# Moving weight loads from the middle of an attention loop to its end, deferring two early loads, and a later turn of V

## The chip, the cores and the metric

One core of a Trainium2 chip runs the whole program. Times are device microseconds of that core. Most executions of one kernel agree within a per cent or two; each run is put down as fast or slow (slow when it is over 1.5% above the fastest of the same kernel), and ratios use fast runs alone. The clock granted to TensorE drops to half (0.50) in some stretches, and the profile shows in which. A profile is one execution, and the profiled one of the kernel before was a slow one (216.32 us, span 214.6).

## The reference

An attention stage feeds a soft mixture of experts:

```python
q, k, v: (8, 8, 576, 64)     beacon_k, beacon_v: (8, 8, 16, 64)
k_all, v_all = concat([beacon, own], axis=2)
a = softmax(causal(q @ k_all.T / 8));  attn = a @ v_all
x = attn.transpose(0, 2, 1, 3).reshape(4608, 512)
logits = x @ phi                       # phi: (512, 32)
slot_input = softmax(logits, 0).T @ x  # 8 experts with 4 slots each
slot_out[e] = relu(slot_input[e] @ w1[e]) @ w2[e]   # w1: (8,512,1024), w2: (8,1024,512)
out = softmax(logits, 1) @ slot_out    # (4608, 512), float32
```

The order matters for the argument: the experts need the softmax over all 4608 tokens, so they can't start before the last head is done, and no row of the output can leave before the last expert is done. The weights, 33.5 MB of 62.7 MB that are read, are needed only there and can be loaded before, as far as there is room: in this kernel the last eight of their 32 pieces lie where q, k and V's tail land, so they can go out only late in the loop.

## The kernel before

Two heads are a pair; a loop runs over 32 pairs, four per batch. Requests for q and k go out on SyncE, those for V and the weights on GpSimd, as V and the weights are cast from 4 to 2 bytes on the way. V comes as a main part per batch and a tail (the last rows of each head, for four batches at once); VectorE has to transpose, or turn, both before they are used. A weight request below is one of 32 pieces, each 1 MB read and 0.5 MB written.

```python
load_pair(0, nc.scalar); ...; load_pair(1); load_pair(2); load_pair(3); load_pair(4)
nc.sync.dma_start(out=phif[:, :, :], in_=moe_phi...)     # 512 pieces of 128 bytes
# ... V of batch 0 and its tail are requested on GpSimd ...
for n in range(NP):
    b, g = divmod(n, H // 2)
    score(n, 0)                      # q.k on TensorE, exp on ScalarE, causal mask on GpSimd
    score(n, 1)
    if n == 0:
        transp(1)                    # TensorE transposes of pair 1, copies on VectorE
        load_pair(5); load_pair(6)
        ...
        turn_v(0, 0); turn_v(0, 1)   # VectorE transposes of V(0): needed by attend(0)
        turn_tail(0, 0); turn_tail(0, 1)
    ...
    if n >= 1:
        attend(n - 1)                # a @ v on TensorE, normalisation on VectorE
    score(n, 2)
    if n + 2 < NP:
        transp(n + 2)
        if n + 7 < NP: load_pair(n + 7)
    score(n, 3)
    if n == 0: beacons(1, B)
    ...                              # requests and turns of the next V
    want = 24 * (n + 1) // 28 if n < 28 else (26, 28, 30, 32)[n - 28]
    while wl < want:
        load_w(wl); wl += 1          # a weight request, on GpSimd
```

Behind the loop come the last normalisation, the last logits, the eight experts (first layer, transposes, second layer), and then nine blocks of output.

The softmax here doesn't subtract the row's maximum and nothing guards it: scores larger than these inputs give would overflow.

Of the kernel before, what the change touches and what calls it, by code (L numbers as in the profile page):

```python
# [17 lines left out]
def kernel(  # L18
# [12 lines left out]
    nc = tc.nc  # L31
    P = 128
    B, H, S, D = q.shape
# [8 lines left out]
    J = S // 64  # L42
# [31 lines left out]
    arena = const.tile([P, E * 8192], F16, name="arena")  # L74
    lend = (E - 2) * 8192
# [9 lines left out]
    def load_pair(n, keng=None, qeng=None):  # L85
        b, g = divmod(n, H // 2)
        for i, (d, src) in enumerate(((qf, q), (kf, k))):
            o = lend + (2 * (n % QKS) + i) * 2 * J * D
            t = arena[:, o:o + 2 * J * D].bitcast(FP).rearrange("p (j d) -> p j d", j=J)
            ((qeng, keng)[i] or nc.sync).dma_start(  # L90
                out=t,
                in_=src[b, 2 * g:2 * g + 2].rearrange("h s d -> (h s) d").rearrange(
                    "(p j) d -> p j d", j=J))
            d[n] = t
# [38 lines left out]
    def turn(dst, src, hf):  # L133
        e = slice(hf * D // 4, (hf + 1) * D // 4)
        nc.vector.transpose(out=dst[:, e],  # L135
                            in_=src.bitcast(FP).rearrange("p (j e) -> p e j", j=TK)[:, e])

    def turn_v(b, hf):
        turn(vh[b % 2].bitcast(FP).rearrange("p c h e -> p e c h" if b == 0 else
                                             "p c h e -> p e h c"), vbuf[b % 2], hf)  # L140

    def turn_tail(b4, hf):
        turn(vt[b4].bitcast(FP).rearrange("p r e -> p e r")[0:96], vlast[0:96], hf)

    def load_bv(b):
        nc.gpsimd.dma_start(out=vbuf[b % 2][0:4 * H:4, 0:Nb * D],
                            in_=beacon_v[b].rearrange("h n d -> h (n d)"))
# [6 lines left out]
    NPC = 4 * E  # L154
# [3 lines left out]
    def load_w(m):  # L158
        e, r = divmod(m, 4)
        if r < 2:  # L160
            src = moe_w1[e, r * 256:(r + 1) * 256].rearrange("(p r) f -> p (r f)", r=2)
        else:
            src = moe_w2[e, (r - 2) * 512:(r - 1) * 512].rearrange("(p r) d -> p (r d)", r=4)
        nc.gpsimd.dma_start(out=arena[:, wloc[m]:wloc[m] + WP], in_=src)  # L164
# [13 lines left out]
    nc.sync.dma_start(out=bkf[:, 1:B, :], in_=bks[:, 1:B, :])  # L178
    load_pair(1)
    load_pair(2)  # L180
    load_pair(3)
    load_pair(4)
    phif = const.tile([P, NDC, NSL], FP, name="phif")
    nc.sync.dma_start(out=phif[:, :, :], in_=moe_phi.rearrange("(c p) e -> p c e", p=P))

    idb = const.tile([P, P], BF, name="idb")
# [6 lines left out]
    idh = const.tile([P, P], F16, name="idh")  # L193
# [26 lines left out]
    def double_beacons(b0, b1):  # L220
        for r in range(2):
            nc.vector.tensor_copy(out=bkd[:, b0:b1, r, :], in_=bkf[:, b0:b1, :])

    def beacons(b0, b1):
        tp = ps_tr.tile([P, B, P], BF, name="tr", tag="tr")
        for b in range(b0, b1):
            nc.tensor.transpose(tp[:, b, :], bkd[:, b, :, :].rearrange("p r d -> p (r d)"),
                                idb[:, :])
        for r in range(2):
            nc.vector.tensor_copy(  # L230
                out=bkT[64 * r:64 * r + 64, b0 * H // 2:b1 * H // 2, :],
                in_=tp[64 * r:64 * r + 64, b0:b1, :].rearrange(
                    "p b (g r n) -> p (b g) r n", g=H // 2, r=2)[:, :, r, :])

    def transp(n):
        (nc.vector if n < 2 else nc.gpsimd).tensor_copy(out=kT[n % 3][:, 0:Nb], in_=bkT[:, n, :])
        for (f, dst) in ((qf, qT[n % 3]), (kf, kT[n % 3])):
            t = f.pop(n)
            tp = ps_tr.tile([P, J, 64], BF, name="tr", tag="tr")
            for j in range(J):  # L240
                for po in (0, 64):
                    hi = t[po:po + 64, j, :].bitcast(BF)[:, 1::2]
                    nc.tensor.transpose(tp[po:po + 64, j, :], hi,  # L243
                                        idb[po:po + 64, po:po + 64])
            nc.vector.tensor_copy(out=dst[:, Nb:Nb + S].rearrange("p (s j) -> p s j", j=J),  # L245
                                  in_=tp[:, :, :].rearrange("p j s -> p s j"))
# [54 lines left out]
    def xt_piece(n):  # L301
        b, g = divmod(n, H // 2)
        if g == 0:
            xT[b] = exq.tile([P, NDC, U], F16, name="xT", tag="xT", bufs=2)
        tp = ps_tr.tile([P, NCH, P], F16, name="tr", tag="tr")
        for i in range(NCH):
            m = P if i < 4 else UL
            nc.tensor.transpose(  # L308
                tp[:, i, 0:m],
                xb[b % 2][0:m, i, 2 * g:2 * g + 2, :].rearrange("p h d -> p (h d)"),  # L310
                idh[0:m, 0:m])
        nc.vector.tensor_copy(out=xT[b][:, g, :],  # L312
                              in_=tp[:, :, :].rearrange("p i u -> p (i u)")[:, 0:U])
# [35 lines left out]
    def add_si(b, hf):  # L349
        sp = si_half(b, hf)  # L350
        z = siacc[:, 2 * hf:2 * hf + 2, :]
        nc.vector.tensor_tensor(out=z, in0=z, in1=sp, op=AL.add)
# [4 lines left out]
    wl = 0  # L357
    for n in range(NP):
        b, g = divmod(n, H // 2)
        score(n, 0)  # L360
        score(n, 1)
        if n == 0:
            transp(1)
            load_pair(5)
            load_pair(6)
            nc.vector.tensor_copy(out=idh[:, :], in_=idb[:, :])
            double_beacons(1, B)
            for hf in range(2):
                turn_v(0, hf)
            for hf in range(2):  # L370
                turn_tail(0, hf)
        if n >= 2:
            xt_piece(n - 2)
        if n >= 5 and g in (1, 2):
            logit_piece(b - 1, g - 1)
        if n >= 6 and g == 3:
            dt_piece(b - 1)
        if n >= 1:
            attend(n - 1)
        if n >= 6 and g == 3:  # L380
            add_si(b - 1, 0)
        if n >= 8 and g == 0:
            add_si(b - 2, 1)
# [3 lines that stand above are left out]
            if n + 7 < NP:  # L387
                load_pair(n + 7)
        score(n, 3)
        if n == 0:  # L390
            beacons(1, B)
        if n == 1:
            nc.vector.tensor_copy(out=phih[:, :, :, :],
                                  in_=phif[:, :, :].unsqueeze(2).broadcast_to([P, NDC, 4, NSL]))

        if n == 1:
            for qd in range(4):
                load_v(1, qd)
        if n == 2:
            load_bv(1)  # L400
        if n == 5:
            nc.gpsimd.memset(siz[:, :, :, :], 0.0)
        if n == 3:
            turn_v(1, 0)
            turn_v(1, 1)
        if 1 <= b < B - 1 and g in (2, 3):
            turn_v(b + 1, g - 2)
        if n == 3:
            for qd in range(4):
                load_v(2, qd)  # L410
        if n >= 4 and b + 2 < B:
            load_v(b + 2, g)
            if g == 0 and b == 1:
                load_bv(2)
            if g == 3:
                load_bv(b + 2)
        if 8 <= n < 11:
            load_tail(1, n - 8)
        if 13 <= n < 15:
            turn_tail(1, n - 13)  # L420
        want = 24 * (n + 1) // 28 if n < 28 else (26, 28, 30, 32)[n - 28]
        while wl < want:
            load_w(wl)
            wl += 1
# [9 lines left out]
    def col_sums(c0, c1):  # L434
# [5 lines left out]
                                scalar2=None, op0=AL.mult)  # L440
        nc.vector.reciprocal(out=z, in_=z)

    L = B - 1
    xt_piece(NP - 2)
    attend(NP - 1, split=True)
# [2 lines left out]
    def last_logits(ts):  # L448
        for hf in range(2):
            for t in ts:  # L450
                o = Nb + hf * (S // 2)
                nc.tensor.matmul(lps[hf], phih[:, t, :, :].rearrange("p g s -> p (g s)"),
                                 xT[L][:, t, o:o + S // 2],
                                 start=(t == 0), stop=(t == NDC - 1))

    add_si(L - 1, 1)
    nc.vector.tensor_scalar(out=siacc[:, :, :], in0=siacc[:, :, :], scalar1=2.0 ** -8,
# [4 lines left out]
    for hf in range(2):  # L462
        o = Nb + L * S + hf * (S // 2)
        nc.scalar.activation(eLh[:, o:o + S // 2], lps[hf], AF.Exp,
                             accum_out=dsum9[:, 2 * L + hf:2 * L + hf + 1])
    col_sums(0, 7)
    dt_piece(L)
    ds = siz[:, :, :, :]
    for hf in range(2):
        sp = si_half(L, hf)  # L470
        for r in range(2):
            c = 2 * hf + r
            nc.vector.scalar_tensor_tensor(
                out=bass.AP(tensor=ds.tensor, offset=ds.offset + c * NSL,
                            ap=[ds.ap[0], [NDC * NSL + SPE, E], [1, SPE]]),
# [106 lines left out]
```

## Time and profile before

The median of the first three runs was 213.8 us (212.13 to 216.71). In the profiled execution:

| point | us |
|---|---|
| first normalisation (pair 0) | 22.64 |
| normalisation of pair 4 | 43.41 |
| normalisation of pair 28 | 157.09 |
| last mask done, last two weight requests | 165.27 |
| second layer of the last expert | 185.92 |
| first output request | 189.55 |
| end of span | 214.6 |

The chain that ended last, from the page (first by engine, then by line):

```profile
PE 40%; DVE 20%; DMA 13%; ACT 10%; issue 5%; POOL 4%; DVEq 0%; POOLq 0%
```

TensorE (PE) is what most of the time is put down to. The table of stretches for points that the argument comes back to (length, busy time and count of PE, PEld (TensorE's weight loads), DVE (VectorE), ACT (ScalarE), POOL (GpSimd), then the granted clock, the DMA share and the GB/s written):

```profile
45.00:125.00 80.00, 69.03 (x1601) 54.04 (x1600) 58.27 (x112) 58.18 (x84) 44.33 (x86) 0.94 1.04 257
125.00:165.30 40.30, 35.03 (x855) 27.16 (x852) 29.64 (x62) 31.36 (x46) 21.63 (x44) 1.00 0.93 193
175.80:189.50 13.70, 11.62 (x181) 5.62 (x180) 3.78 (x13) 3.78 (x9) 0.00 (x0) 0.88 0.01 1
```

For 13.7 us ahead of the first output request the DMA engines have nothing to do, as all weights are there and no output is ready.

### The profile page before, as it was taken

How to read it: one execution, taken by the hardware profiler on the slowest of the kernel's cores; microseconds unless marked ns; L12 is line 12 of the kernel's file. 1: busy time of each engine (PE TensorE's matmuls, PEld its weight loads, DVE VectorE, ACT ScalarE, POOL GpSimd, SP SyncE). 2: the span in 40 equal slices, each digit the busy share in tenths (PEclk: the TensorE clock that was granted, in tenths of full speed). 3: DMA queues.
4: the chain of work that ended last, by engine and by line, in shares of the span. 5: the costliest groups of instructions: out<-in, count | busy, mean ns of one | idle time of the engine just before them, and what ended most of it. 6: DMA issues, size and time to landing. Idle time of an engine off the chain costs nothing.

```text
span 214.6 us, 7759 instructions
## 1 busy us (share of the span) xinstructions
PE 160.2 (75%) x3400; PEld 117.0 (55%) x3400; DVE 136.1 (63%) x284; ACT 128.5 (60%) x188; POOL 92.1 (43%) x180
## 2 busy tenths in 40 slices
PE   1545992998799869788959898789897889788200
PEld 1424762776577657676748677666675654333000
DVE  4477783579767849985766578579755442289400
ACT  2322893587688668568935896687887212289300
POOL 8500985585558655544544366533566000000000
PEclk9999998599999999979985999999999958999955
DMA  6998499999999999999999979998799950059997
GB/s 189 292 298 324 89 244 262 267 259 259 280 260 246 260 269 261 281 250 256 219 259 253 234 191 234 246 241 128 132 195 208 218 118 3 0 220 415 415 415 293
DMA packets 20273, 50.88 MB, mean 237 GB/s; under 512 B 5392, under 2 KB 5392, under 8 KB 19216
## 3 DMA queue, kind: packets, MB, share of 16 engines
q0 software_dynamic: 8000, 21.75, 53.7%
q1 hardware_dynamic: 12096, 28.35, 36.3%
q8 instruction: 26, 0.43, 0.7%
q10 hardware_dynamic: 144, 0.29, 0.4%
q14 instruction: 7, 0.06, 0.1%
HBM read 62.69 MB, written 9.44 MB: 336 GB/s over the span
## 4 chain that ended last, share of the span: by engine, by line
PE 40%; DVE 20%; DMA 13%; ACT 10%; issue 5%; POOL 4%; DVEq 0%; POOLq 0%
PE av L283 11%; ACT ex L262 10%; PE sc L256 9%; DMA vbuf<-in_v_dram 5%; DVE arena L546 5%; DMA arena<-in_v_dram 5%; PE tr L308 4%; DVE xb L294 4%; PE tr L243 4%; DMA vbuf<-in_beacon_v_dram 3%; DVE vh L135 3%; PE tr L319 3%; PE av L515 2%; DVE xT L312 2%; DVE kT L245 1%
## 5 line engine op out<-in xcount | busy, mean ns | idle before, releaser
L262 ACT ACTIVATE ex<-sc 128x1024 f16<-128x1024 f32 (+3 forms) x128 | 105.8, 870 | 52.4 <-PE sc L256 49.9
L264 POOL TENSOR_SCALAR_AFFINE_SELECT ex<-ex 128x1024 f16<-128x1024 f16 x32 | 35.4, 1106 | 67.5 <-ACT ex L262 67.5
L256 PE MATMUL sc<-qT,kT 64*128 64x128 bf16 (+5 forms) x576 | 46.5, 259 | 9.5 <-ACT ex L262 6.8
L283 PEld LDWEIGHTS <-ex 128*128 128x128 f16 (+2 forms) x960 | 37.6, 109 | 5.7 <-issue 4.6
L283 PE MATMUL av<-vh,ex 128*128 128x65 f16 (+1 forms) x896 | 38.6, 201 | 1.8 <-issue 1.6
L243 PE MATMUL tr<-idb,arena 64*64 64x64 bf16 x1152 | 29.5, 202 | 10.6 <-DVE xT L312 4.1
L243 PEld LDWEIGHTS <-arena 64*64 64x64 bf16 x1152 | 24.4, 116 | 19.1 <-issue 14.2
L256 PEld LDWEIGHTS <-kT 64*128 64x128 bf16 (+1 forms) x576 | 22.0, 103 | 19.3 <-issue 15.0
L294 DVE TENSOR_TENSOR xb<-av,r 128x640 f16<-128x640 f32 (+1 forms) x33 | 26.5, 804 | 1.1
L245 DVE COPY qT<-tr 128x576 bf16<-128x576 bf16 x32 | 24.0, 750 | 4.2 <-PE tr L243 4.0
L245 DVE COPY kT<-tr 128x576 bf16<-128x576 bf16 x32 | 24.0, 749 | 2.9 <-PE tr L243 2.8
L293 DVE RECIPROCAL r<-av 128x10 f32<-128x10 f32 (+1 forms) x33 | 7.2, 217 | 26.3 <-PE av L283 26.2
L135 DVE STREAM_TRANSPOSE vh<-vbuf 128x512 f32<-128x512 f32 x16 | 17.8, 1131 | 4.5 <-DMA vbuf<-in_beacon_v_dram 3.5
L312 DVE COPY xT<-tr 128x592 f16<-128x592 f16 x32 | 14.5, 453 | 9.1 <-PE tr L308 8.9
L164 POOL DMA_DIRECT2D arena<-in_moe_w_dram x32 | 18.0, 564 | 0.0
L111 POOL DMA_DIRECT2D vbuf<-in_v_dram x28 | 15.9, 576 | 2.6 <-DVE xT L312 2.6
L308 PE MATMUL tr<-idh,xb 128*128 128x128 f16 (+1 forms) x160 | 14.6, 225 | 1.0 <-DVE xb L294 1.0
L308 PEld LDWEIGHTS <-xb 128*128 128x128 f16 (+1 forms) x160 | 9.5, 101 | 7.2 <-issue 5.6
L546 DVE TENSOR_SCALAR arena<-fp,rc 128x512 f32<-128x512 f32 x18 | 12.3, 746 | 0.7 <-PE fp L542 0.7
L542 PE MATMUL fp<-soh,eLh 128*128 128x512 f16 x36 | 10.6, 377 | 2.6 <-ACT arena L544 1.3
L544 ACT ACTIVATE arena<-fp,rc 128x512 f32<-128x512 f32 x18 | 11.3, 686 | 1.7 <-PE fp L542 1.0
L319 PE MATMUL tr<-xT,phih 128*128 128x288 f16 x56 | 10.6, 295 | 1.1 <-DVE xT L312 1.1
(74 smaller groups left out, 130.5 us busy)
## 6 DMA issues: line engine op xcount, KB each, us to landing
arena<-in_moe_w_dram POOLq DMA_DIRECT2D x32, 512.0 KB, 9.6
arena<-in_q_dram SPq DMA_DIRECT2D x32, 288.0 KB, 8.8
arena<-in_k_dram SPq DMA_DIRECT2D x31, 288.0 KB, 10.6
out_dram<-arena SPq DMA_DIRECT2D x8, 1024.0 KB, 8.5
vbuf<-in_v_dram POOLq DMA_DIRECT2D x31, 128.0 KB, 7.4
out_dram<-arena SPq DMA_DIRECT2D x2, 512.0 KB, 3.1
arena<-in_v_dram POOLq DMA_DIRECT2D x4, 128.0 KB, 8.1
arena<-in_k_dram ACTq DMA_DIRECT2D x1, 288.0 KB, 2.7
```

Source lines behind the costliest of these rows:

```text
L135: nc.vector.transpose(out=dst[:, e], in_=src.bitcast(FP).rearrange("p (j e) -> p e j", j=TK)[:, e])
L164: nc.gpsimd.dma_start(out=arena[:, wloc[m]:wloc[m] + WP], in_=src)
L243: nc.tensor.transpose(tp[po:po + 64, j, :], hi, idb[po:po + 64, po:po + 64])
L245: nc.vector.tensor_copy(out=dst[:, Nb:Nb + S].rearrange("p (s j) -> p s j", j=J), in_=tp[:, :, :].rearrange("p j s -> p s j"))
L256: nc.tensor.matmul(sc[0:kn, a, col:col + un], kT[n % 3][64 * a:64 * a + 64, P * c:P * c + kn], qT[n % 3][64 * a:64 * a + 64, u0:u0 + un], ...
L262: nc.scalar.activation(ex[n][:, :, o:o + w], sc[:, :, 0:w], AF.Exp, scale=scale)
L264: nc.gpsimd.affine_select(out=ex[n][:, :, 0:512].rearrange("p a (c t) -> p a c t", c=4), in_=ex[n][:, :, 0:512].rearrange("p a (c t) -> p ...
L283: nc.tensor.matmul(av[0:m, a, i * DD:(i + 1) * DD], ex[n][0:kn, a, o:o + m], vchunk(b, 2 * g + a, c, kn), start=(c == 0), stop=(c == i))
L294: nc.vector.tensor_tensor(out=xo[:, z], in0=avv[:, z, :, 0:D], in1=r_.unsqueeze(3).broadcast_to([P, z.stop - z.start, NCH, D]), op=AL.mult)
L308: nc.tensor.transpose(tp[:, i, 0:m], xb[b % 2][0:m, i, 2 * g:2 * g + 2, :].rearrange("p h d -> p (h d)"), idh[0:m, 0:m])
L312: nc.vector.tensor_copy(out=xT[b][:, g, :], in_=tp[:, :, :].rearrange("p i u -> p (i u)")[:, 0:U])
L546: nc.vector.tensor_scalar(out=osb[:, j, :], in0=fp_[:, :], scalar1=rc[:, i:i + 1], scalar2=None, op0=AL.mult)
```

## The change

Its intent: fill that hole. Of the 32 weight requests only 11 go out while q, k and V still load (before: 20 by pair 23), 11 more in the last eight pairs, and ten behind the loop. At the start, pairs 3 and 4 are held back until the first mask is done (two tiny memsets on GpSimd write the target, so the load must wait for them), to let V(0) in sooner; and VectorE turns V(0) only after pair 2's copies and the beacons.

```diff
-    load_pair(3)
-    load_pair(4)
     phif = ...; nc.sync.dma_start(out=phif[:, :, :], ...)
@@ n == 0, behind score(0, 1)
             transp(1)
+            nc.vector.tensor_copy(out=idh[:, :], in_=idb[:, :])
+            for m in (3, 4):
+                o = lend + 2 * m * 2 * J * D
+                nc.gpsimd.memset(arena[:, o:o + 2 * J * D + 2:2 * J * D], 0.0)
+                load_pair(m)
             load_pair(5)
             load_pair(6)
-            nc.vector.tensor_copy(out=idh[:, :], in_=idb[:, :])
             double_beacons(1, B)
-            turn_v(0, 0..1); turn_tail(0, 0..1)        # (loops written short)
@@ n == 0, behind score(0, 3)
             beacons(1, B)
+            turn_v(0, 0..1); turn_tail(0, 0..1)
@@
-        want = 24 * (n + 1) // 28 if n < 28 else (26, 28, 30, 32)[n - 28]
+        want = n if n < 4 else 3 + 42 * (n - 3) // 100 if n < 24 else 11 + 145 * (n - 23) // 100
@@ behind the loop
+    while wl < NPC:
+        load_w(wl)
+        wl += 1
     L = B - 1
```

More of the change, by code (lines that the diff above doesn't have):

```diff
@@ L363 @@
             transp(1)
+            nc.vector.tensor_copy(out=idh[:, :], in_=idb[:, :])
[3 more added lines that the diff above has]
+                load_pair(m)
             load_pair(5)
             load_pair(6)
-            nc.vector.tensor_copy(out=idh[:, :], in_=idb[:, :])
             double_beacons(1, B)
-            for hf in range(2):
-                turn_v(0, hf)
-            for hf in range(2):
-                turn_tail(0, hf)
         if n >= 2:
@@ L391 @@
             beacons(1, B)
+            for hf in range(2):
+                turn_v(0, hf)
+            for hf in range(2):
+                turn_tail(0, hf)
         if n == 1:
```

## The prediction

> **What bounds the kernel now.** I read the page first (busy tenths, queues), then the chain of waits, then the timelines of VectorE and GpSimd, and last a table of stretches cut at the points those showed. The busy tenths of the page, by slices of 5.4 us:
>
> ```profile
> PEclk9999998599999999979985999999999958999955
> DMA  6998499999999999999999979998799950059997
> GB/s 189 292 298 324 89 244 262 267 259 259 280 260 246 260 269 261 281 250 256 219 259 253 234 191 234 246 241 128 132 195 208 218 118 3 0 220 415 415 415 293
> ```
>
> The DMA engines are at 8 tenths or more nearly everywhere, with two holes: slice 5 (20 to 25 us), and slices 33 to 35 (about 175 to 189 us), where no weights are left to load and no output is ready. The change aims at both. GB/s are bytes written; V and the weights are cast from 4 to 2 bytes on the way, so 208 to 218 GB/s of weights alone means 416 to 436 read.
>
> The stretches (columns: length, then busy time and count of PE, PEld, DVE, ACT, POOL, then the clock, the DMA share and GB/s):
>
> ```profile
> 20.00:25.00 5.00, 4.79 (x108) 3.72 (x105) 3.00 (x7) 4.11 (x5) 3.72 (x8) 1.00 0.36 79
> 43.40:157.10 113.70, 98.42 (x2340) 76.83 (x2340) 84.68 (x165) 83.99 (x120) 63.15 (x123) 0.95 1.00 238
> 165.30:175.00 9.70, 7.33 (x147) 5.49 (x143) 4.89 (x22) 2.63 (x7) 1.05 (x2) 0.86 1.02 205
> 175.00:189.50 14.50, 12.42 (x193) 6.10 (x190) 3.96 (x13) 4.16 (x10) 0.00 (x0) 0.86 0.01 2
> 189.50:214.60 25.10, 9.30 (x32) 3.38 (x30) 11.51 (x17) 10.33 (x17) 0.00 (x0) 0.77 0.91 376
> ```
>
> 43.4 to 157.1 us are the 24 pairs between the normalisations of pair 4 and pair 28: DMA is full, but TensorE is also busy 98.4 of 113.7 us. To tell which of them sets the pace I took the starts of that normalisation (one per pair) from VectorE's timeline: four pairs take 18.2, 18.9, 19.5, 21.2, 18.1 and 17.7 us. In the last of these six batches the steps are 4.2, 4.0, 4.3 and 5.2 us, and TensorE's waits there are fractions of a microsecond on ACT and VectorE. So about 17.7 us a batch is the compute pace, and the 24 pairs lose 113.7 - 6 x 17.7 = 7.5 us to everything else: about 1 us is two tail turns, some 3.5 us the half-clock stretches at 87 and 108 us, and 2 to 3 us DMA (late V, instruction fetches of TensorE).
>
> The start is different. VectorE's timeline:
>
> ```profile
> 13.63 2.03 DVE L135 STREAM_TRANSPOSE vh<-vbuf 128x512 f32<-128x512 f32 x2 [0.94 <-DMA vbuf<-in_v_dram]
> 16.03 2.02 DVE L135 STREAM_TRANSPOSE arena<-arena 96x512 f32<-96x512 f32 x2 [0.37 <-DMA arena<-in_v_dram]
> 17.92 0.73 DVE L245 COPY qT<-tr 128x576 bf16<-128x576 bf16 x1
> 22.64 0.83 DVE L294 TENSOR_TENSOR xb<-av,r 128x640 f16<-128x640 f32 x1
> 35.44 2.08 DVE L135 STREAM_TRANSPOSE vh<-vbuf 128x512 f32<-128x512 f32 x2 [3.53 <-DMA vbuf<-in_beacon_v_dram]
> ```
>
> The turns of batch 0's V sit in VectorE's order ahead of pair 2's q/k copies, so the copies wait for V and its tail until 17.92, and the first normalisation comes at 22.64. Then the turn of V(1) waits 3.53 us for a beacon piece. GpSimd, which issues V and weights in its program order, shows why, and where the last weights go out:
>
> ```profile
> 28.32 0.56 POOL L146 DMA_DIRECT2D vbuf<-in_beacon_v_dram  x1 [0.97 <-DMA vbuf<-in_v_dram]
> ...
> 165.27 1.07 POOL L164 DMA_DIRECT2D arena<-in_moe_w_dram  x2
> ```
>
> **What the Trainium skill says.** "DMA: Bandwidth & Descriptors", Specifications, gives a fabric ceiling of 435 GB/s over 16 engines; the weights-only slices here (218 written, 436 read) and the output (415) agree. Its section on the anatomy of a SWDGE DMA says that DMA engines do not wait on semaphores, the issuing sequencer does: the trace agrees, GpSimd sat idle 0.97 us in front of the beacon request, its masks behind it. The same page, "Issuing engines are not separate DMA queues", says that all issuers share the 16 engines, so deferring weights and pairs 3 and 4 should speed V. "TensorE: Matmul & The Clock Gate" says that the array falls to half clock after an idle window of about 3.4 us; the trace has half-clock stretches of 6.8 us at 32.6, 107.7 and 169.1, the first in the 4.15 us idle at the V(1) turn. Fewer stalls may mean fewer such stretches.
>
> **The change, part by part.**
> (1) Turns of V(0) later. Bytes read by 16.1 us: q/k of pairs 0 to 4 2.95 MB, beacon keys 0.26, V(0) and tail 1.84, that is 5.05 MB in 14.1 us, 358 GB/s. Without pairs 3 and 4 (1.18 MB) what the start needs is 3.87 MB, 10.8 us, landing near 13 us instead of 16. Pair 2's copies then end near 14.5, the turns (4.05 us) near 18.5 to 20, and the first normalisation near 19.3 to 21: 1.7 to 3.3 us earlier. V(1) is requested after pair 1's mask, whose scores no longer wait for the turns: near 16.5 instead of 22.77.
> (2) Pairs 3 and 4 wait for two tiny memsets on GpSimd behind pair 0's masks (end 10.05 us), so they are asked for near 10 us; pair 3 is transposed near 20, so there is slack. The memsets (0.1 us each) cost nothing on the path.
> (3) V(1)'s beacon piece: before, request to turn took 5.5 + 7.1 us and cost 3.53. V(1) now starts about 6.3 us earlier against a need 2.5 us earlier, but into a DMA queue still holding pairs 3 to 6, say 1.5 us lost: the stall falls to about 1.2. Saving 2.3.
> (1) to (3) make pair 4 about 4.8 us earlier.
> (4) Fewer weights in pairs 4 to 24 (42 per 100 pairs instead of 86): up to the 2 to 3 us of DMA waits, and perhaps 1 to 2 us of half clock that follow them: 3.5 us.
> So the last masks and with them the last requests come G = 4.8 + 3.5 = 8.3 us earlier (165.3 becomes 157).
> (5) The cost. Before, four weights or so were in flight at 165.3; they landed by 175, and the experts ended 187.0, bound by TensorE. Now only 22 of 32 are requested inside the loop, the 22nd at 157, and ten behind it. One weight is 0.524 MB written; at 213 GB/s 2.46 us. Two requests at the pair before (161.1 - G, 1.5 us start, 2 x 2.5) keep the engines until 167.6 - G; eleven more are 27.1 us: the last lands at 194.7 - G + 0.5 = 186.9. The last second layer and its wait take 0.9, then soh and output, in the profile 187.0 to 214.6, 27.6 us. End: 186.9 + 0.9 + 27.6 = 215.4 against 214.6. The experts are now bound by the landing of weights, about 9 us behind where TensorE could be; that eats G.
> The output (9.44 MB at 415 GB/s, 22.7 us) is unchanged.
>
> **Rivals.**
> A: the DMA queue is the bound through the whole loop, as its share of 1.00 suggests, and relief speeds every pair; then G is 11 to 13 and the span 210 to 212. For it: share 1.00, the late V. Against: 17.7 us a batch with TensorE nearly gapless.
> B: V(1) and V(2) still come late, as requests bunch in the first 20 us; G is 5 and the span 218.7. For it: pairs 3 to 8 now load exactly while V(1) does.
> C: the tail is hidden, as the experts' own work of 14 us takes as long as the weights. That needs landing by 186 - G, and 11 weights at 2.46 us rule it out unless fewer remain than I count.
> My sum lies between A and B.
>
> **Range and chances.** The profiled run was a slow one: 216.3 us for a span of 214.6, against a median of 213.8. Its half clock at 169 to 176 lies in the experts' stage and would be hidden in the changed kernel, behind weights. So I carry over 1.7 us from span to time (217.1) and take off half of the 2.5 us between this run and the median, about 215.9. The odd constants (42 and 145 per 100) look like ones found by trying on a chip, which speaks for a gain that I can't derive, so I lower this to 214.0. The 8-in-10 range is 209.5 to 218.5: G from 5 to 13, with the clock's share. Over 2% faster needs less than 209.5, thus rival A in full: 0.10. Over 2% slower needs more than 218.1, thus rival B: 0.13. Within 2%: 0.77.
>
> **What would show it right or wrong.** First normalisation at 19 to 21 us; the wait for V(1)'s beacon piece at 0 to 2 us; a batch of four pairs near 17.7 us with a DMA share near 0.8 between 45 and 125 us; the 22nd weight requested near 157 and the last weight landing near 187; DMA full from there back to 157; TensorE idle in the experts' stage, waiting for weights; no DMA hole ahead of the output of more than about 4 us. The prediction is wrong if batches fall well below 17.7 us, if weights land faster than 2.4 us each, or if the start saves more than 6 us or nothing.

## The result, and the profile after

| | median | range | runs |
|---|---|---|---|
| before, beside the changed kernel | 214.74 us | 212.13 to 216.71 | 4 |
| changed | 221.45 us | 220.35 to 224.0 | 4 |

The ratio is 1.037 (95% interval 1.025 to 1.049): slower, outside the predicted range. A ratio here is the mean time of one kernel's fast runs over that of the other's fast runs of the same rounds, so it is not quite the ratio of the medians.

The busy tenths of the changed kernel's page, by slices of 5.5 us:

```profile
PEclk9999999999999999999999999999995875579955
DMA  6998999999999988976998799999999999259995
GB/s 178 275 295 320 144 221 266 244 266 263 198 233 200 256 193 241 199 215 171 246 213 220 193 215 218 171 186 195 189 181 214 212 214 212 58 214 425 414 417 242
```

The hole ahead of the output has shrunk to about one slice, as intended, and this profile has no half-clock dips inside the loop. But from slice 11 to slice 27 the GB/s are mostly 170 to 250, where they were 220 to 280 before. The chain that ended last now has another first entry:

```profile
DMA 31%; PE 26%; DVE 15%; ACT 10%; issue 7%; POOL 5%; SPq 1%; DVEq 1%; ACTq 0%; POOLq 0%
```

DMA has taken TensorE's place, and by line half of it (16% of the span) is waiting for weights. The stretches, with the same columns as before:

```profile
45.00:125.00 80.00, 69.73 (x1728) 53.97 (x1726) 63.00 (x124) 61.29 (x89) 44.56 (x88) 1.00 0.90 219
125.00:158.20 33.20, 29.17 (x698) 22.75 (x697) 23.30 (x49) 26.60 (x39) 16.83 (x33) 1.00 0.99 197
158.20:190.60 32.40, 20.49 (x325) 11.02 (x322) 7.72 (x32) 5.32 (x14) 5.80 (x12) 0.71 1.00 197
190.60:194.90 4.30, 2.95 (x11) 0.94 (x11) 1.24 (x3) 1.59 (x3) 0.00 (x0) 0.50 0.00 0
```

The hole went from 13.7 to 4.3 us. In its place stands the third row: 32.4 us between the last mask and the landing of the last weight, where the kernel before took 10.5. TensorE is busy 20.5 us of it, much of that at half clock. How TensorE waited in the experts' stage (timeline of TensorE):

```profile
176.62 0.61 PE L520 MATMUL av<-arena,hbuf 128*32 128x512 f16 x8
183.50 0.62 PE L503 MATMUL av<-arena,siz 128*32 128x256 f16 x8 [6.26 <-DMA arena<-in_moe_w_dram]
185.99 0.62 PE L503 MATMUL av<-arena,siz 128*32 128x256 f16 x8 [1.88 <-DMA arena<-in_moe_w_dram]
...
190.87 1.04 PE L520 MATMUL av<-arena,hbuf 128*32 128x512 f16 x6 [0.95 <-DMA arena<-in_moe_w_dram]
```

L503 is the first layer, L520 the second. The bracket gives the idle time and what ended it: three times it is a weight, and the last expert's second half starts at 190.87.

Where did the weights go? The DMA view of the same 80 us in the middle of the loop, first before, then after (packets; then per queue packets, MB written, share of 16 engines; q0 is GpSimd's, with V and weights, q1 is SyncE's, with q and k):

```profile
DMA packets 8632, 20.57 MB, mean 257 GB/s; under 512 B 1744, under 2 KB 1744, under 8 KB 8616
q0 software_dynamic: 3803, 10.46, 68.0%
q1 hardware_dynamic: 4813, 9.87, 35.4%
```

```profile
DMA packets 8085, 17.54 MB, mean 219 GB/s; under 512 B 1779, under 2 KB 1779, under 8 KB 8067
q0 software_dynamic: 2826, 6.56, 49.0%
q1 hardware_dynamic: 5241, 10.72, 39.9%
```

q0's bytes count twice on the reading side, because of the cast. So before, 2 x 10.46 + 9.87 = 30.8 MB were read in 80 us, 385 GB/s; after, 2 x 6.56 + 10.72 = 23.8 MB, 298 GB/s. That is 7.0 MB less, and at the 2 x 213 = 426 GB/s that weights reach alone it is 16.4 us of work put off to the end, to fill a hole of 13.7. What the loop gained in return was 5.5 us between the normalisations of pairs 4 and 28, as it was near TensorE's pace already. The share fell only from 1.04 to 0.90: it counts time in which packets are under way, not bytes. The Trainium skill says, in "Perfetto Trace Analysis", section "Identifying the Most-Contended Engine", that for DMA one should use the HBM utilization (the throughput) instead of occupancy, as 16 engines make occupancy misleading. This trace agrees (a share of 0.99 at 197 GB/s, mostly of weights, from 125 to 158 us, where weights alone reach 213). The prediction called the loop's DMA full by the share of 1.00; by bytes it was at 385 of 426 GB/s between 45 and 125 us.

### The profile page after: what moved, and what is told of

Read it like the earlier page. It is cut to its first block, busy times and chain, and to the rows that moved or that the text cites.

```text
span 220.6 us, 7771 instructions
## 1 busy us (share of the span) xinstructions
PE 161.0 (73%) x3400; PEld 114.7 (52%) x3400; DVE 135.8 (62%) x284; ACT 128.6 (58%) x188; POOL 91.6 (42%) x182
## 4 chain that ended last, share of the span: by engine, by line
DMA 31%; PE 26%; DVE 15%; ACT 10%; issue 7%; POOL 5%; SPq 1%; DVEq 1%; ACTq 0%; POOLq 0%
DMA arena<-in_moe_w_dram 16%; ACT ex L260 9%; DMA arena<-in_k_dram 9%; PE av L281 7%; PE sc L254 7%; DMA vbuf<-in_v_dram 6%; PE tr L241 4%; DVE vh L135 3%; POOL ex L262 3%; PE tr L306 2%; DVE arena L551 2%; DVE xb L292 2%; DVE kT L243 2%; PE fp L547 2%; PE tr L317 2%
## 5 line engine op out<-in xcount | busy, mean ns | idle before, releaser
L254 PE MATMUL sc<-qT,kT 64*128 64x128 bf16 (+5 forms) x576 | 45.6, 253 | 9.8 <-ACT ex L260 7.1
L281 PEld LDWEIGHTS <-ex 128*128 128x128 f16 (+2 forms) x960 | 36.7, 108 | 6.7 <-issue 5.7
L281 PE MATMUL av<-vh,ex 128*128 128x65 f16 (+1 forms) x896 | 37.6, 199 | 2.1 <-DVE vh L135 2.0
L241 PE MATMUL tr<-idb,arena 64*64 64x64 bf16 x1152 | 28.6, 200 | 9.6 <-DMA arena<-in_q_dram 5.2
L241 PEld LDWEIGHTS <-arena 64*64 64x64 bf16 x1152 | 23.6, 114 | 18.2 <-DMA arena<-in_q_dram 8.5
L254 PEld LDWEIGHTS <-kT 64*128 64x128 bf16 (+1 forms) x576 | 21.4, 101 | 19.6 <-issue 15.3
L292 DVE TENSOR_TENSOR xb<-av,r 128x640 f16<-128x640 f32 (+1 forms) x33 | 26.5, 804 | 1.1
L164 POOL DMA_DIRECT2D arena<-in_moe_w_dram x32 | 17.6, 556 | 6.9 <-DMA arena<-in_moe_w_dram 6.8
L310 DVE COPY xT<-tr 128x592 f16<-128x592 f16 x32 | 14.4, 450 | 8.1 <-PE tr L306 8.1
L306 PE MATMUL tr<-idh,xb 128*128 128x128 f16 (+1 forms) x160 | 14.1, 220 | 1.0 <-DVE xb L292 1.0
L514 DVE COPY hbuf<-tr 128x256 f16<-128x256 f16 x8 | 2.3, 292 | 19.2 <-PE tr L513 19.2
L547 PE MATMUL fp<-soh,eLh 128*128 128x512 f16 x36 | 11.6, 426 | 2.6 <-ACT arena L549 1.5
```

What stands on the lines that cost most here:

```text
L164: nc.gpsimd.dma_start(out=arena[:, wloc[m]:wloc[m] + WP], in_=src)
L241: nc.tensor.transpose(tp[po:po + 64, j, :], hi, idb[po:po + 64, po:po + 64])
L254: nc.tensor.matmul(sc[0:kn, a, col:col + un], kT[n % 3][64 * a:64 * a + 64, P * c:P * c + kn], qT[n % 3][64 * a:64 * a + 64, u0:u0 + un], ...
L281: nc.tensor.matmul(av[0:m, a, i * DD:(i + 1) * DD], ex[n][0:kn, a, o:o + m], vchunk(b, 2 * g + a, c, kn), start=(c == 0), stop=(c == i))
L292: nc.vector.tensor_tensor(out=xo[:, z], in0=avv[:, z, :, 0:D], in1=r_.unsqueeze(3).broadcast_to([P, z.stop - z.start, NCH, D]), op=AL.mult)
L306: nc.tensor.transpose(tp[:, i, 0:m], xb[b % 2][0:m, i, 2 * g:2 * g + 2, :].rearrange("p h d -> p (h d)"), idh[0:m, 0:m])
```

## The experiments

All outputs are right. The kernels of a group (e1 to e4, e5 to e8, e9 to e11, and e12 alone) ran on the same chip beside the same runs of the kernel before.

| run | what | median us | ratio (95%) |
|---|---|---|---|
| e1 | new weight schedule alone | 225.24 | 1.055 (1.047 to 1.063) |
| e2 | both changes at the start, old schedule | 211.24 | 0.982 (0.970 to 0.993) |
| e3 / e12 | V turned later alone | 211.05 / 209.23 | - / 0.983 (0.973 to 0.993) |
| e4 | pairs 3 and 4 deferred alone | 214.92 | 0.998 (0.984 to 1.011) |
| e6 | changed kernel, 21 weights all within the last eight pairs | 215.0 | 0.998 (0.987 to 1.010) |
| e7 | changed kernel, phi requested later | 221.76 | - |
| e8 | V later; 15 + 17 weights | 210.45 | 0.985 (0.976 to 0.994) |
| e9 | V later; old pace to 22, ten behind | 216.82 | 1.016 (1.007 to 1.025) |
| e10 | V later; 13 + 19 weights | 209.3 | 0.978 (0.971 to 0.986) |
| e5 / e11 | V later; 16 + 11 + 5 weights | 209.52 / 209.87 | - / 0.979 (0.971 to 0.988) |

A dash stands where too few runs were fast for a ratio; e3 and e5 were repeated for that reason. By the medians of all runs, fast and slow, the ratios are 1.049 (e1), 1.010 (e9), 1.008 (e6), 1.001 (e4), 0.987 (e8), 0.984 (e2), 0.978 (e11), 0.975 (e10) and 0.970 (e12); the changed kernel has 1.031. That is the same order but for e12.

**Theory and rival.** Theory T: the tail is the loss; weights still to be requested behind the last mask cost 2.5 us of DMA each, and the end follows them. Rival S: the loss is at the start, where the profile showed the first normalisation at 24.22 us instead of 22.64.

**e1, the weight schedule alone.** The new `want` line and the requests behind the loop, put into the kernel before:

```diff
-        want = 24 * (n + 1) // 28 if n < 28 else (26, 28, 30, 32)[n - 28]
+        want = n if n < 4 else 3 + 42 * (n - 3) // 100 if n < 24 else 11 + 145 * (n - 23) // 100
@@ behind the loop
+    while wl < NPC: load_w(wl); wl += 1
```

> The kernel before with the new weight schedule alone (11 in the first 24 pairs, 21 in the last eight and behind). Theory T (the tail is the loss: ten weights requested behind the last mask land about 32 us later and the end follows 30 us behind that): last request near 160, as the loop gains the 5 us or so that it gained in the changed kernel, last landing near 192, time 7 to 10 us over the kernel before (ratio 1.03 to 1.045), so as slow as the whole change or slower. Rival S (the loss is at the start, where the first normalisation came 1.6 us later): ratio 0.99 to 1.01.

Measured 225.24 us, ratio 1.055. S is out: without the changes at the start the schedule costs more than the whole change did. T's ratio was up to 1.045, so it fell short by a per cent; the last weight was used at 194.53 us in that profile. Its first normalisation came at 24.18 us, with the start of the kernel before: so the 24.22 of the changed kernel is no sign of what the change did there.

**e2, the start alone.** The other two parts of the change, with the old schedule.

> The kernel before with the two changes at the start (pairs 3 and 4 behind the first mask, V turned later) and the old weight schedule. Theory T: the first normalisation late at 24 us, but the wait for V(1) gone, so 0 to 2 us faster than before (ratio 0.99 to 1.00). Rival S: 3 us or more slower (ratio over 1.015).

Ratio 0.982: the start helps, on the mean by more than T's 0 to 2 us. The first normalisation was at 21.77, not 24.22, in this profile.

**e3 and e12, V turned later alone.**

```diff
@@ n == 0, behind score(0, 1)
-            turn_v(0, 0..1); turn_tail(0, 0..1)
@@ n == 0, behind beacons(1, B)
+            turn_v(0, 0..1); turn_tail(0, 0..1)
```

> The kernel before with V turned later alone. If the late first normalisation of the changed kernel comes from deferring pairs 3 and 4 (rival D), it is here at 20 to 21.5 us and the time 1 to 3 us below before (ratio 0.985 to 0.995). If it comes from the later turns themselves, it is at 23 to 25 us here too and the time within 1 us of before or above.

> The kernel with V turned later alone once more, as too few of its runs were in the fast state for a ratio. If the later turn alone gives what both changes at the start gave together (0.982), the deferral of pairs 3 and 4 is worth nothing: ratio 0.975 to 0.99, and the wait of VectorE for V(1)'s beacon piece is absent again. If the deferral carried part of it: 0.99 to 1.0.

e3 gave 211.05 us with one fast run, e12 0.983. VectorE's timeline in e12:

```profile
15.54 2.06 DVE L135 STREAM_TRANSPOSE vh<-vbuf 128x512 f32<-128x512 f32 x2
17.47 2.01 DVE L135 STREAM_TRANSPOSE arena<-arena 96x512 f32<-96x512 f32 x2
20.91 0.82 DVE L294 TENSOR_TENSOR xb<-av,r 128x640 f16<-128x640 f32 x1
30.81 2.12 DVE L135 STREAM_TRANSPOSE vh<-vbuf 128x512 f32<-128x512 f32 x2
```

The turns start later than the 13.63 us of the kernel before and yet the first normalisation is earlier (20.91 against 22.64), because pair 2's copies no longer stand behind them; and the last line has no bracket, where V(1)'s turn had waited 3.53 us. That wait is absent in the profile of every kernel that turns V later, and present in the three that don't (before 3.53, e4 2.81, e1 1.65). This part alone gives all that e2 gave.

**e4, the deferral alone.**

> The kernel before with pairs 3 and 4 deferred alone. Rival D: pair 1's k lands at 13 to 14 us as in the changed kernel (10 us before), and the first normalisation is no earlier than 22.6; time 0 to 3 us over before. If deferring frees the DMA engines for V as the prediction said: the turn of V starts at 12 to 13 us without a wait and the first normalisation comes at 19.5 to 21, time 1 to 3 us below before.

Ratio 0.998 (0.984 to 1.011): no gain shown. V(0)'s turn started at 14.16 us, the tail's at 16.06, and neither had to wait, but that is no earlier than in the kernel before (13.63 and 16.03); pair 1's copies came later (its k at 12.34 us, 10.78 before), and the first normalisation was at 22.72, as ever:

```profile
11.06 0.76 DVE L243 COPY qT<-tr 128x576 bf16<-128x576 bf16 x1 [4.23 <-PE tr L241]
12.34 0.76 DVE L243 COPY kT<-tr 128x576 bf16<-128x576 bf16 x1 [0.52 <-PE tr L241]
14.16 2.03 DVE L135 STREAM_TRANSPOSE vh<-vbuf 128x512 f32<-128x512 f32 x2
```

The DMA view of the first 12 us, over all profiles, shows what deferring did for V: its tail landed 8.6 to 10.3 us after the request in the five profiles with pairs 3 and 4 deferred, 9.5 to 11.7 in the nine without, about 1.3 us sooner on the mean; V(0)'s main part was no sooner (8.7 to 10.1 against 8.3 to 9.6). Whether pair 1 pays for it isn't shown: its k was copied at 10.2 to 14.4 us with the deferral and at 10.2 to 12.1 without.

**e7, is it phi?** With pairs 3 and 4 gone from the front of SyncE's queue, phi's load of 512 small pieces moved up behind pair 2. Here it is requested behind pair 6.

```diff
     phif = const.tile([P, NDC, NSL], FP, name="phif")
-    nc.sync.dma_start(out=phif[:, :, :], ...)
@@ n == 0
             load_pair(6)
+            nc.sync.dma_start(out=phif[:, :, :], ...)
```

> The changed kernel with the load of phi (512 pieces of 128 bytes), which the change moved up to directly behind pair 2 in SP's queue, requested behind pair 6 instead. If these small packets[...] hold up pairs 1 to 4 (theory P): pair 1's k is there by 10 to 11 us instead of 13.7, the first normalisation at 20.5 to 22 instead of 24.2, time 2 to 3.5 us under the changed kernel (ratio to before 1.015 to 1.03). If deferring pairs 3 and 4 does it by giving V more turns, nothing moves: 24 us, ratio 1.035 to 1.04.

This one failed to settle anything. Pair 1's k was copied at 11.89 us and the first normalisation came at 22.15, which fits theory P; but e2 and e6, with phi in its early place and the same start, had 11.85 and 10.23, 21.77 and 21.09, and e1, with the old start, had its first normalisation at 24.18. So the 24.22 of the changed kernel's profile was largely that execution, not the code. With a median of 221.76 no gain shows, and a single fast run gives no ratio.

**e6, the same 11, but all others within the loop.** Where does the pace of the last requests come in?

```diff
-        want = ... else 11 + 145 * (n - 23) // 100
+        want = ... else 11 + 21 * (n - 23) // 8
```

> The changed kernel with 11 weights in the first 24 pairs as it has, but the other 21 all requested within the last eight pairs and none behind them. Theory T (too slow a pace of requests, 1.45 per pair, and ten left over): the DMA engines take the 21 weights back to back from pair 24 on (about 115 us), 21 x 2.5 = 52 us plus the last q/k, last landing 175 to 180, time 204 to 211, ratio 0.95 to 0.985. Rival R (the bytes are the bound: the engines showed a share of 0.99 in those pairs already): last landing stays at 187 or later, ratio 1.02 or more.

Ratio 0.998, 6 us better than the changed kernel, but between T and R. The stretches of its profile:

```profile
45.00:125.00 80.00, 70.74 (x1757) 55.08 (x1754) 64.52 (x127) 62.37 (x89) 44.92 (x88) 1.00 0.90 221
125.00:181.30 56.30, 43.72 (x916) 30.40 (x915) 26.76 (x72) 28.06 (x48) 20.25 (x38) 0.94 1.03 210
```

From 125 us to the last landing at 181.3 the engines now write 210 GB/s, nearly all of it weights, without a break, and still that ends 4 us after TensorE could have used it. No pace of requests helps any more: the bytes that were not moved between 45 and 125 us (221 GB/s there, as in the changed kernel) are missing. Compare e2, which has the same start and the old schedule: 0.982 against 0.998, with intervals that overlap, so that the thin stream in the middle seems to cost 1.6%. The slow pace with ten behind the loop brings 0.998 to 1.037, and there the intervals are apart. So T, as I had put it, was about half of it.

**e9, the other half alone.** A thick stream in the middle, and ten behind, with V turned later:

```diff
-        want = 24 * (n + 1) // 28 if n < 28 else (26, 28, 30, 32)[n - 28]
+        want = min(24 * (n + 1) // 28, 22)
@@ behind the loop
+    while wl < NPC: load_w(wl); wl += 1
```

> V turned later, the first 22 weights at the pace of the kernel before (so the stream in the middle of the loop stays as thick as before), none from pair 26 on, and ten behind the last mask as in the changed kernel. This separates the two halves of the loss. If the ten behind cost what the prediction said, 2.46 us each from an empty queue: last mask near 159, last landing 159 + 1.5 + 25 = 186, end 186 + 30 = 216 us of span, time 217, 6 us over the kernel with V turned later alone, ratio 1.01 to 1.025. If only the thin stream in the middle hurts: 209 to 212, ratio 0.975 to 0.99.

Measured 216.82 us, ratio 1.016, with the last weight in at 185.9 us and a span of 215.3: T's landing, span and time to a microsecond. In part that is luck: the last mask came 1.2 us before T's 159, and the ten took 1.6 us longer than T's 26.5.

```profile
125.00:157.80 32.80, 28.59 (x692) 22.35 (x691) 22.60 (x48) 25.91 (x38) 12.78 (x25) 1.00 0.39 94
157.80:185.90 28.10, 19.84 (x325) 10.93 (x322) 7.70 (x32) 5.31 (x14) 5.29 (x11) 0.81 0.96 189
```

The engines idle ahead of the last mask (94 GB/s) and then take 28.1 us for the ten. Against V turned later alone (0.983) the ten cost some 3.3%, about 7 us.

**e5, e8, e10, e11: schedules between.** All have V turned later and pairs 3 and 4 as before.

```diff
# e5, e11
+        want = n if n < 4 else 3 + 65 * (n - 3) // 100 if n < 24 else 16 + 145 * (n - 23) // 100   # 5 behind
# e8
+        want = n if n < 4 else 3 + 60 * (n - 3) // 100 if n < 24 else 15 + 17 * (n - 23) // 8
# e10
+        want = n if n < 4 else 3 + 50 * (n - 3) // 100 if n < 24 else 13 + 19 * (n - 23) // 8
```

> V turned later, pairs 3 and 4 loaded as before, and a weight schedule between the two: 16 in the first 24 pairs, 27 by the last pair, five behind it. Theory T (what hurts is the number of weights still to be requested behind the last mask, 2.5 us of DMA each): last request near 159, five behind it land about 20 us later, just where TensorE gets to the last expert, so no loss in the tail: ratio to before 0.97 to 0.985. Rival: any weight moved out of the loop costs its 2.5 us at the end: ratio 1.00 or more.

> V turned later, pairs 3 and 4 as before, 15 weights in the first 24 pairs and the other 17 within the last eight, none behind. Theory T: the loop loses its DMA waits (2 to 3 us against the kernel with V turned later alone), the last weight lands about 175, before TensorE needs it: time 206 to 210, ratio 0.96 to 0.98. Rival R as in the run before: ratio over 1.0.

> V turned later, pairs 3 and 4 as before, 13 weights in the first 24 pairs and 19 within the last eight, none behind. Between the run with 11 and 21 (last landing 181, loop ends 153) and that with 15 and 17 (landing 175, loop ends 160). Landing and TensorE should meet here near 176 to 178: time 205 to 209, ratio 0.96 to 0.98. If it is no better than the run with 15 and 17 (0.985), the optimum is flat and decided by the clock.

> The kernel with 16, 11 and 5 weights again, with more rounds, as its first runs were mostly put in the slow state: 205 to 210 us, ratio 0.965 to 0.985, if its one fast run was no accident.

e10 and e11 gave 0.978 and 0.979, e8 0.985. All three beat the kernel before and the changed one, but their intervals overlap with that of V turned later alone (0.973 to 0.993), so that the schedule adds anything to the later turn is not shown. In e5 and e11 the five weights behind the loop cost nothing that shows: no wait on a weight stands in the experts' stage of their profiles, as e5's theory T had it. e10 met its own target: the last weight was in at 177.9 us and TensorE waited 1.46 us for it.

```profile
125.00:177.90 52.90, 44.61 (x963) 31.43 (x957) 28.60 (x76) 29.80 (x50) 20.14 (x38) 0.94 1.02 212
177.90:182.00 4.10, 2.56 (x13) 1.02 (x13) 1.93 (x4) 2.13 (x4) 0.00 (x0) 1.00 0.00 0
```

So the landing can be matched to TensorE and the hole closed to 4.1 us, and the prize over the later turn alone, half a per cent by the means, is within the noise. e8's loop was slower than e10's in its profile (its last normalisation of a whole pair at 160.6 us, 155.4 in e10), with a half-clock dip from about 153 us.

## Why the prediction was wrong

The mechanism stood on record: "The experts are now bound by the landing of weights, about 9 us behind where TensorE could be; that eats G." The step that failed is (5): the sum sized the time from the last mask to the landing of the last weight at 29.9 us, and it took 32.4. To that came a discount at the end that no view supported. The predicted span was 215.4, the measured 220.6, and the 5.2 us fall on three terms:

| term of the sum | predicted | measured | miss |
|---|---|---|---|
| G, the last mask earlier (165.3 minus) | 8.3 | 7.1 (158.2) | 1.2 |
| last mask to landing of the last weight | 186.9 - 157.0 = 29.9 | 190.6 - 158.2 = 32.4 | 2.5 |
| from there to the end | 28.5 | 220.6 - 190.6 = 30.0 | 1.5 |

**Step (5), the tail.** The sum has this term too short for every profile with the new schedule: from the last mask to the use of the last weight it takes 32.7 us in the changed kernel, 32.8 in e1, 32.3 in e7. The stretches show where:

```profile
158.20:160.00 1.80, 1.24 (x25) 0.89 (x22) 1.23 (x3) 1.35 (x2) 1.80 (x5) 1.00 1.09 221
160.00:164.00 4.00, 2.99 (x59) 2.24 (x57) 2.19 (x7) 0.48 (x3) 2.41 (x5) 1.00 0.94 168
164.00:188.00 24.00, 14.35 (x239) 7.51 (x236) 4.00 (x21) 3.48 (x11) 1.59 (x3) 0.67 1.06 214
188.00:190.60 2.60, 1.92 (x16) 0.38 (x13) 0.29 (x1) 0.00 (x0) 0.00 (x0) 0.50 0.40 79
```

The rate for a full stream was right: 214 GB/s from 164 to 188 us is 2.45 us a weight. What the sum lacked are the two ends: 4 us at 168 GB/s behind the last mask, worth 0.9 us, and a last stretch of 2.6 us in which a share of 0.40 of the engines still worked on the rest, worth 1.6 us where 0.5 had been allowed: together 2.0 of the 2.5 us. e1, e7, e9 and e10 end in the same way (40, 77, 67 and 58 GB/s in their last 1.6 to 2.8 us). Why the rate dips at 160 to 164 us is not settled.

- **From there to the end.** In e10, at full clock where the changed kernel had half (row 177.90 to 182.00 above), this takes 207.2 - 177.9 = 29.3 us. So the half clock (0.71 and 0.50 in the last rows of the stretches after) can account for at most 0.7 of the 1.5 us; the rest was sized too small. "TensorE: Matmul & The Clock Gate" of the Trainium skill, as the prediction cited it, fits only in part: one half-clock stretch of the changed kernel begins at 179.0 us, within the wait of 6.26 us that ends at 183.50, but the one before begins at 165.3 with no wait over 0.71 us ahead of it. The prediction's own times for the kernel before are some 3 us early: by the windows the half clock begins at 35.7, 110.8 and 172.3 us, also at 90.4, and of these only the first lies in a wait as long as 3.4 us.
- **G, steps (1) to (3).** Pair 4 was 1.6 us earlier (41.83 against 43.41), not 4.8. Much of that is this one execution: with the same start, pair 4 was 2.1, 4.7 and 4.2 us earlier in e2, e6 and e7, and the last mask of e7, whose code differs only in phi's place, was done at 154.5 us, a G of 10.8. So these runs don't show that the 1.2 us of this term belong to the code. In part step (1) was wrong: deferring pairs 3 and 4 brought V's tail about 1.3 us sooner and not 3, and e4 shows no gain. The later turn was right in kind: 0.983 alone, and step (3)'s wait for V(1) was gone altogether.
- **G, step (4).** Pairs 4 to 28 took 150.03 - 41.83 = 108.2 us, 5.5 less than before; predicted were 3.5. In this stretch the six batches took 17.6 to 18.5 us, three of them 17.6 to 17.8, the compute pace, with a granted clock of 1.00 throughout. Rival A, that the loop would go far below that, was rightly refused: in e7, whose G comes near A's 11 to 13, the batches take 17.6 to 18.5 us too.
- **What would have shown the trade sooner.** The sum did count the weights left for the end. Bytes read per stretch show the trade without a sum: 16.4 us of loading taken from a loop that hardly waited for it, against a hole of 13.7 us. e6 and e9 look at these two halves one by one.
- **The discount.** The sum gave 217.1 us with the clock as profiled, and 3.1 were taken off, 1.9 of them because the constants "look like ones found by trying on a chip". No view supported that, and it moved the range's upper end to 218.5. Together with the 5.2 above, less the 0.9 by which the profiled run lay over the median (222.36 against 221.45), this is the whole miss: 5.2 + 3.1 - 0.9 = 7.4 of 7.45 us.

Against rival B (G of 5, span 218.7) the G of the profiled run was between B and the sum, and the end still later than B's. Rival C was refused for the right reason.

Left open: why the rate dipped at 160 to 164 us; whether phi's place matters at all; and how much of the start's spread between executions of the same code (pair 1's k copied at 10.2 to 14.4 us) comes from the DMA engines.

## What to carry to other kernels

Before filling a hole in the DMA queue with loads from elsewhere, ask what the place they leave will do with the room: if the loop there is paced by an engine, its stream only gets thinner, and the same bytes come back at the end, one after the other, on the path. A few can be moved, as long as the last of them lands before it is asked for (e10, e11). Count bytes read per stretch against the rate of the best stretch, not the busy share. And test the parts of a combined change one by one: here one part gave 1.7%, one nothing that shows, and one took more than 5%, which together is the 3.7% of the whole.

## What the Trainium skill lacked or had wrong

- "DMA: Bandwidth & Descriptors", Specifications and Bandwidth: its 435 GB/s ceiling and the 425 that it measured for a single core agree with this trace. But under "Where 436 GB/s comes from" it says that for transfers between HBM and SBUF the HBM side, about 358 GB/s, binds: this program, on one core, read its weights at 2 x 7.38 MB in 35 us, 422 GB/s (e10, 140 to 175 us). It does not say which side counts in a casting DMA: here 214 GB/s were written with the cast from 4 to 2 bytes, 414 to 425 in the uncast output, so the wider side, the reading one, fits the rate.
- No page that I read says how many requests GpSimd can have open: in the changed kernel it issued eight weight requests in a row at 158.16 us, then waited 3.02, 1.90 and 1.92 us before each of the last three, for earlier weights to land; in e9, from an empty queue, the ninth and the tenth waited 1.12 and 2.17 us. Whether the chip or the program's own semaphores set this limit is not shown.
- "Perfetto Trace Analysis" warns of DMA occupancy but gives no measure of the error: here a stretch with a share of 0.99 wrote 197 GB/s and one with 1.02 wrote 212, both weights for the most part.
